# Cutting the last q loads of the first batch finer: 4, 4, 4, 2, 2 rows per partition in place of 8, 4, 2, 2

## Chip, cores and metric

The kernel runs on one core of a Trainium2 chip. The metric is the device time of one execution in microseconds (us); a median over several executions is quoted. A ratio is the mean time of one kernel's fast runs over that of the other's fast runs of the same rounds, so it is not quite the ratio of the medians beside it. "Span" is the time from the first to the last instruction in a profile; it is 1.8 us shorter than the device time.

## The reference

Two stages follow each other. Per batch (4 of them, 6144 rows, 256 columns), q and k are normed over the rows, their 256 x 256 product goes through a softmax, and v is multiplied by it. The result goes through a feed-forward stage with three input matrices and a maximum.

```python
qn = q / (norm(q, axis=1) + 1e-06);  kn = k / (norm(k, axis=1) + 1e-06)
a = softmax(kn.transpose(0, 2, 1) @ qn / tau)
x = (v @ a).reshape(B * S, D)
out = maximum(maximum(x @ w1, x @ w2), x @ w3) @ w_out
```

## The kernel before

The kernel multiplies the softmax matrix into w1, w2 and w3 first (tiles `aw`), so that v needs only one matmul per piece of the hidden layer (`h_ps`, L389) and one for the output (`o_ps`, L409). All this can start only when the first batch's softmax is known, and that needs all of its q and k. So the start of the kernel is a load stage: GpSimd issues the loads (they cast float32 to fp8 on the way), and the TensorE follows them. Sixteen DMA engines carry a load in sixteen parts, here called its shares, and a load has "landed" when its last share has. "Gram" is the product of q and k, and "backlog" is the matmuls that already have their data and still wait for their turn. Lines left out of the code are marked by dots.

```python
HEAD = 8
...
SP.dma_start(out=kf, in_=k_r[0][:, 0:HEAD, :])
for load, widths in ((load_k, [8] * 5), (load_q, [8] * 5 + [4, 2, 2])):
    g0 = HEAD if load is load_k else 0
    for w in widths:
        load(0, g0, w)          # POOL.dma_start of w rows per partition
        g0 += w
        ...
...
load_v(0)
...
for fp in range(d_ff // FT):
    load_w(fp)                  # three loads each: w1, w2, w3
```

The gram of the first batch reads q in pairs of rows; a matmul waits for the load that its rows came with. A pair of rows is two steps (j) of two matmuls:

```python
def gram(b):
    ...                                          # L165: k times k, 24 row pairs
    for tp in range(NG // 2):
        tsl = slice(2 * tp, 2 * tp + 2)
        ...
        for j in range(CC):
            ...
            PE.matmul(ps[j][:, 0:C], lhsT=qt[:, tsl, jsl], rhs=kt[:, tsl, :], ...)           # L177
            PE.matmul(ps[j][:, C:C + P], lhsT=qt[:, tsl, jsl], rhs=qt[:, tsl, jsl], ...)     # L179
```

After it come six warm-up matmuls (L469), the softmax on VectorE and ScalarE, the transposes of the first v (L372), the first products with w (L335), and then the first h matmul (L389), from where the TensorE works without a break:

```python
products(0, (0, 1))     # first half of the softmax matrix with w1, then with w2
sums(0); sums(1)
...
products(1, (0, 1))     # second half
for j in range(CC):
    products(j, (2,))   # w3
```

## Time and profile before

| | |
|---|---|
| time, median of the first three runs | 574.29 us (574.02 to 574.39) |
| the run that was profiled | 574.48 us, span 572.7 |
| TensorE busy | 97% of the span |
| idle before rows 32 to 39 of q | 2.04 us |
| gram of the first batch ends | 34.82 us |
| first h matmul (L389) starts | 38.09 us |

The prediction below shows the lines. How to read them: everything of interest happens in the first 38 us, where the TensorE follows the loads; after 38 us it waits for nothing.

### The profile page before, as it was taken

To read this page: it belongs to the slowest core of one execution; us is meant where nothing else is said; L and a number is where in the kernel's file an instruction comes from. 1 tells how busy PE (TensorE), PEld (TensorE's weight loads), DVE (VectorE), ACT (ScalarE), POOL (GpSimd) and SP (SyncE) were. 2 spreads that over 40 slices of the span, in tenths; PEclk is the share of its full clock that TensorE was granted. 3 is DMA by queue.
4 is the path that set the end of the run, shared out by engine and by line. 5 is a ranking of instruction groups with operands and counts; after the bars stand their busy time and mean duration, and the time that the engine had idled before them with its cause. 6 is when DMAs were issued, how large, how long until landed. Compare 5 with 4: busy or idle time off the path is not lost.

```text
span 572.7 us, 9441 instructions
## 1 busy us (share of the span) xinstructions
PE 553.5 (97%) x3349; PEld 330.8 (58%) x3350; DVE 411.0 (72%) x647; ACT 309.0 (54%) x539; POOL 234.5 (41%) x239
## 2 busy tenths in 40 slices
PE   3789999999999999999999999999999999999997
PEld 2665555555755555555575555555575555555566
DVE  0048777777577778777768777777868778778775
ACT  1044567767455476776545467767645444444443
POOL 2432257776740077777560048777750000000000
PEclk9999999999999999999999999999999999999999
DMA  9997998885699168885179339885537333132112
GB/s 142 106 146 124 139 236 129 152 139 108 110 107 159 57 101 160 134 145 115 58 128 149 94 82 143 155 134 93 130 79 160 75 74 111 56 101 66 56 56 76
DMA packets 76816, 65.64 MB, mean 115 GB/s; under 512 B 52448, under 2 KB 62304, under 8 KB 76640
## 3 DMA queue, kind: packets, MB, share of 16 engines
q0 software_dynamic: 18928, 26.48, 38.8%
q1 hardware_dynamic: 57696, 38.41, 23.7%
q8 instruction: 26, 0.43, 0.3%
q14 instruction: 22, 0.18, 0.1%
q10 hardware_dynamic: 144, 0.13, 0.1%
HBM read 78.64 MB, written 25.17 MB: 181 GB/s over the span
## 4 chain that ended last, share of the span: by engine, by line
PE 94%; DMA 2%; issue 2%; POOL 1%; DVE 0%; POOLq 0%
PE h_ps L389 65%; PE o_ps L409 22%; PE gram L260 3%; PE ew_ps L311 3%; DMA q_sb<-in_q_dram 2%; POOL k_sb L99 0%; PE o_ps L434 0%; POOL q_sb L102 0%; PE gram L177 0%; PE ew_ps L335 0%; PE warm_ps L469 0%; PE gram L179 0%; PE vt_ps L372 0%; PE n_ps L215 0%; DVE ht_sb L395 0%
## 5 line engine op out<-in xcount | busy, mean ns | idle before, releaser
L389 PE MATMUL h_ps<-vt_sb,aw_sb 128*128 128x512 bf16 (+1 forms) x1764 | 406.7, 375 | 0.1
L389 PEld LDWEIGHTS <-aw_sb 128*128 128x128 bf16 x1764 | 171.8, 98 | 161.3 <-DVE aw_sb L317 2.0
L394 DVE TENSOR_TENSOR s_mx<-h_ps,s_mx 128x512 bf16<-128x512 f32 (+1 forms) x294 | 198.7, 676 | 87.2 <-ACT s_mx L393 86.9
L393 ACT ACTIVATE s_mx<-h_ps 128x512 bf16<-128x512 f32 (+1 forms) x294 | 172.3, 586 | 124.9 <-PE h_ps L389 124.0
L395 DVE TENSOR_TENSOR ht_sb<-h_ps,s_mx 128x512 bf16<-128x512 f32 (+1 forms) x294 | 200.2, 681 | 31.4 <-PE o_ps L409 0.5
L203 POOL TENSOR_TENSOR acc<-acc,sq 128x768 f32<-128x768 f32 x90 | 147.6, 1650 | 70.7 <-ACT sq L197 63.1
L409 PE MATMUL o_ps<-wo_sb,ht_sb 128*128 128x256 bf16 x1128 | 153.9, 273 | 0.0
L409 PEld LDWEIGHTS <-ht_sb 128*128 128x128 bf16 x1128 | 110.4, 98 | 52.0
L412 ACT ACTIVATE o_sb<-o_ps 128x512 f32<-128x512 f32 x94 | 56.1, 597 | 85.4 <-PE o_ps L409 85.4
L110 POOL DMA_DIRECT2D v_sb<-in_v_dram x48 | 27.4, 576 | 36.5 <-DMA vt_sb<-v_sb 35.4
L197 ACT ACTIVATE sq<-q_sb 128x768 bf16<-128x768 fp8e4 x48 | 40.5, 844 | 0.0
L197 ACT ACTIVATE sq<-k_sb 128x768 bf16<-128x768 fp8e4 x48 | 40.1, 835 | 0.0
L200 POOL CAST acc<-sq 128x768 f32<-128x768 bf16 x6 | 4.9, 821 | 69.5 <-ACT sq L197 69.5
L102 POOL DMA_DIRECT2D q_sb<-in_q_dram x32 | 17.9, 567 | 4.5 <-DMA v_sb<-in_v_dram 2.5
L165 PE MATMUL kk<-k_sb 128*128 128x256 fp8e4 x48 | 7.5, 338 | 12.2 <-DVE k_sb L151 6.4
L99 POOL DMA_DIRECT2D k_sb<-in_k_dram x29 | 16.1, 556 | 2.1 <-DMA v_sb<-in_v_dram 1.3
L260 PE MATMUL gram<-k_sb,q_sb 128*128 128x512 fp8e4 x144 | 16.8, 276 | 0.0
L260 PEld LDWEIGHTS <-q_sb 128*128 128x256 fp8e4 x144 | 15.9, 136 | 0.6
L314 ACT ACTIVATE aw_sb<-ew_ps,rinv 128x384 bf16<-128x384 f32 (+1 forms) x24 | 13.1, 554 | 5.6 <-PE ew_ps L311 4.7
L311 PE MATMUL ew_ps<-w_sb,et 128*128 128x384 bf16 (+1 forms) x96 | 15.6, 313 | 0.0
L177 PE MATMUL gram<-k_sb,q_sb 128*128 128x512 fp8e4 x48 | 11.3, 334 | 3.2 <-DMA q_sb<-in_q_dram 3.2
L165 PEld LDWEIGHTS <-k_sb 128*128 128x256 fp8e4 x48 | 6.4, 182 | 13.2 <-DMA k_sb<-in_k_dram 6.7
(67 smaller groups left out, 113.1 us busy)
## 6 DMA issues: line engine op xcount, KB each, us to landing
out_dram<-o_sb SPq DMA_DIRECT2D x41, 512.0 KB, 2.9
v_sb<-in_v_dram POOLq DMA_DIRECT2D x48, 256.0 KB, 4.2
k_sb<-in_k_dram POOLq DMA_DIRECT2D x24, 192.0 KB, 5.7
q_sb<-in_q_dram POOLq DMA_DIRECT2D x24, 192.0 KB, 7.1
out_dram<-o_sb SPq DMA_DIRECT2D x13, 256.0 KB, 2.0
k_sb<-in_k_dram POOLq DMA_DIRECT2D x5, 256.0 KB, 11.1
q_sb<-in_q_dram POOLq DMA_DIRECT2D x5, 256.0 KB, 10.4
w_sb<-in_moe_w_dram POOLq DMA_DIRECT2D x9, 128.0 KB, 5.5
```

Source lines behind the costliest of these rows:

```text
L102: POOL.dma_start(out=qk[b][0][:, g0:g0 + w, :], in_=q_r[b][:, g0:g0 + w, :])
L110: POOL.dma_start(out=t, in_=v_r[gi // NCH, gi % NCH])
L197: ACT.activation(out=sq, in_=src, func=AF.Square)
L203: POOL.tensor_tensor(out=acc, in0=acc, in1=sq, op=ALU.add)
L260: PE.matmul(g[:, j * C:(j + 1) * C], lhsT=qt[:, tsl, j * P:(j + 1) * P], rhs=kt[:, tsl, :], start=(tp == 0 and j == 0), stop=(tp == NG // ...
L311: PE.matmul(ew[:, :w], lhsT=et[:, j, ic * P:(ic + 1) * P], rhs=w_sb[m][:, j, fsl], start=(j == 0), stop=(j == CC - 1))
L389: PE.matmul(t.rearrange("p (t n) -> p t n", n=P), lhsT=aw[m][:, ic, fsl], rhs=vt[:, tsl, ic, :], start=(ic == 0), stop=(ic == CC - 1))
L393: ACT.activation(out=s_mx, in_=hp[0], func=AF.Copy)
L394: DVE.tensor_tensor(out=s_mx, in0=hp[1], in1=s_mx, op=ALU.max)
L395: DVE.tensor_tensor(out=ht, in0=hp[2], in1=s_mx, op=ALU.max)
L409: PE.matmul(st["ps"][:, half], lhsT=ht[:, fc, t * P:(t + 1) * P], rhs=wo_sb[:, fc, :], start=(fc == 0), stop=(fc == FC - 1))
L412: ACT.activation(out=st["o"][:, t - 1:t + 1, :].rearrange("p t d -> p (t d)"), in_=st["ps"], func=AF.Copy)
```

## The change

The last loads make the TensorE wait for whole loads. The intent is to let it begin on rows 32 to 35 while rows 36 to 39 are still under way, so that less work is left when the last rows land.

```diff
-    for load, widths in ((load_k, [8] * 5), (load_q, [8] * 5 + [4, 2, 2])):
+    for load, widths in ((load_k, [8] * 5), (load_q, [8] * 4 + [4, 4, 4, 2, 2])):
```

## The prediction

> **What bounds the kernel now.** I read the page first, then the chain of work, then the timeline of the TensorE around the loads that the change touches, then the time from issue to landing of each single load.
>
> The page says that the TensorE is busy nearly all the time, and the chain that ended last puts 94% of the span on it and only 2% on a DMA: the wait for `q_sb`, the tensor whose loads are cut differently.
>
> ```profile
> PE 553.5 (97%) x3349; PEld 330.8 (58%) x3350; DVE 411.0 (72%) x647; ACT 309.0 (54%) x539; POOL 234.5 (41%) x239
> ...
> PE 94%; DMA 2%; issue 2%; POOL 1%; DVE 0%; POOLq 0%
> ```
>
> The same chain, in order of time, shows where those 2% lie: one piece of 13.48 us ahead of the gram matmuls of the first batch, ending at 31.88.
>
> ```profile
> 18.40 13.48 DMA q_sb<-in_q_dram
> 31.88 0.05 issue
> 31.93 0.32 PE gram L177
> ```
>
> The piece starts where the load was issued. The load itself waits in a queue behind other loads, so 13.48 us is no saving on offer. What the TensorE loses is read from its timeline, here with start, length and, in brackets, the idle time before:
>
> ```profile
> 29.67 0.22 PE L179 MATMUL gram<-q_sb 128*128 128x256 fp8e4 x1
> 31.93 0.32 PE L177 MATMUL gram<-k_sb,q_sb 128*128 128x512 fp8e4 x1 [2.04 <-DMA q_sb<-in_q_dram]
> ```
>
> It has used up rows 0 to 31 of q at 29.7 and idles 2.04 us for rows 32 to 39, the last load of 8 rows. After that it waits for nothing more: the same view shows it working from 31.93 to the end of the gram matmuls at 34.82. The waits of the TensorE after 38 us come out as an empty list, so what is won or lost before 38 us reaches the end of the kernel one to one, and nothing else is on offer.
>
> The landings, each from the view of DMA issues over a window that holds one issue only (size, then us from issue to landing): the load of rows 32 to 39, then those of 4, 2 and 2 rows, issued at 18.40, 18.92, 19.44 and 19.96.
>
> ```profile
> q_sb<-in_q_dram POOLq DMA_DIRECT2D x1, 256.0 KB, 13.5
> ...
> q_sb<-in_q_dram POOLq DMA_DIRECT2D x1, 128.0 KB, 13.5
> ...
> q_sb<-in_q_dram POOLq DMA_DIRECT2D x1, 64.0 KB, 13.6
> ...
> q_sb<-in_q_dram POOLq DMA_DIRECT2D x1, 64.0 KB, 13.7
> ```
>
> To a hundredth, from the trace's landing records: rows 24 to 31 at 28.29, 32 to 39 at 31.88, 40 to 43 at 32.42, 44 to 45 at 33.02, 46 to 47 at 33.67. Every 8-row load up to there came 2.4 to 2.5 us after the one before it; this one came 3.59 us after. The per-engine records of its landing explain that: fifteen of its sixteen shares landed between 29.82 and 30.74, and one at 31.88. At 29.88 a single packet of another queue started and took 0.97 us; the window from 29.85 to 30.9 has it:
>
> ```profile
> q8 instruction: 1, 0.02, 5.8%
> ```
>
> It is a block of instructions for the TensorE (working below), and one of the sixteen DMA engines carried it in the middle of its share of rows 32 to 39.
>
> **What the Trainium skill says.** "Runtime: NRT & Kernel Launch", section Instruction fetch mechanics: an engine's instructions come in blocks of 16 KiB, 256 instructions, over the sequencer's own DMA queue. The trace agrees: queue q8 moved 26 packets of 16,384 bytes, and 3349 + 3350 TensorE instructions over 256 make 26.2. "DMA: Bandwidth & Descriptors", section Why a DMA increments its semaphore by 16 and not by 1: a load counts as landed only when all sixteen engines have reported; the 15 + 1 shares above are just that. The same page, section Anatomy of one DMA, gives each DMA a fixed cost of about 2.0 us, mostly completion latency. This trace shows that it is not paid in series when loads queue up: the first of the sixteen shares of consecutive loads landed at 27.36, 29.82, 31.10, 31.75 and 32.39, so 8 rows took 2.46 us, 4 rows 1.28, 2 rows 0.65 and 0.64. "TensorE: Matmul & The Clock Gate", Part 1, says that the array runs at half clock until it has been busy for a few microseconds. The trace agrees: a step of two gram matmuls took 0.32 us until 26.77 and 0.167 us after, and stayed fast over the 2.04 us of idling.
>
> **The change, part by part.** One load of 8 rows becomes two of 4; the rest is as before. The order of instructions shows one more DMA issue on GpSimd (240 rows against 239), none added elsewhere, and the other engines' order unchanged apart from which of the eight DMA semaphores each wait names.
>
> *Removed.* The matmuls for rows 32 to 35 no longer wait for rows 36 to 39. Rows 32 to 35 need 1.28 us after the shares of the load before. The latest share of that one was at 28.29, so they land by about 29.57, before the instruction block at 29.88 can delay them. The TensorE runs out at 29.7, so it goes straight on. A pair of rows takes two steps of two matmuls, so rows 32 to 47 are 16 steps, 2.67 us from 31.93 to 34.60 (0.167 each), and rows 32 to 35 are 4 steps, 0.67 us. So 0.67 us of work moves from after 31.93 to before 30.4, into idle time.
>
> *Added.* One DMA. On an engine 8 rows cost 2.46 us, twice 4 rows 2.56: 0.10 us later for everything behind it in the queue, rows 36 to 39 at about 31.98, then 32.52, 33.12 and 33.77. On GpSimd one more issue, about 0.57 us; it issues that far ahead of the landings that this is hidden. With eight semaphores in turn, a load waits for the one eight before it, so the first load of v and the first three of w are issued one landing later (v at 23.4 in place of 21.2); their turn at the DMA engines comes only after 33.7, so this is hidden as well.
>
> *The gram's end.* From 31.98 + 0.05: rows 36 to 39 until 32.70, rows 40 to 43 (there at 32.52) until 33.37, rows 44 to 45 (33.12) until 33.70, rows 46 to 47 at 33.77 + 0.05, with 0.34 us of work, until 34.16, and 0.06 more of draining. Against 34.82 that is 0.6 us earlier. The end is now set by the last landing and not by the backlog.
>
> *What follows it.* Six warm-up matmuls, the transposes of v, the softmax, and the first matmuls with w. Here the timeline reads:
>
> ```profile
> 35.96 0.61 PE L372 MATMUL vt_ps<-ident,v_sb 128*128 128x128 bf16 x8
> 36.50 0.61 PE L335 MATMUL ew_ps<-w_sb,et 128*128 128x256 bf16 x4
> 36.94 0.24 PE L329 MATMUL rs_ps<-ones_c,et 128*128 128x1 bf16 x4
> 37.05 1.03 PE L335 MATMUL ew_ps<-w_sb,et 128*128 128x256 bf16 x8
> ```
>
> These come 0.6 us earlier only if their data is there. v landed at 35.00 for 35.96 (0.96 us to spare); the first w at 35.66 for 36.50 (0.84); the second at 36.31 for the third of those four matmuls, at 36.73 (0.42); the third at 36.96 for 37.48 (0.52). All of them come 0.10 later now. The tightest is the second w: 0.42 - 0.10 leaves 0.32 us. So of the 0.6 us the TensorE keeps about 0.3 and gives the rest back in a wait for w that is not there now. **Sum:** 574.29 - 0.3 = 574.0.
>
> **The rivals.** *The gain arrives whole (573.7).* It would if the second w came earlier than I reckon, for instance if splitting costs nothing on the DMA engines or the share that is late there has caught up. Against it: those loads run back to back, the DMA engines are full (the table of windows gives a DMA share of 1.05 and 1.20 for 25 to 30 and 30 to 35 us), and nothing in the change makes them faster. *A wait takes the place of the wait (574.3 or a little more).* If the split costs 0.3 us and more, or the instruction block strikes the first of the two loads or the last ones, the last rows land later and all is lost. Speaking for it: one packet moved a landing by 1.1 us here. Against it: what calls for that block is the TensorE's progress up to 29.7, which does not change. *The 2 us of the fixed cost are paid again (576).* The spacings of 0.65 us between loads of 2 rows speak against it. *The array falls back to half clock (575 to 576).* The idle stretches become shorter, not longer, so I give it little. *The wait was worth its 2.04 us (572.3).* That would need the last landing to move, which it doesn't: splitting brings nothing sooner than 33.67.
>
> **Range and chances.** The three runs of before spread 0.37 us, and my gain may be 0.0 to 0.65 with a centre at 0.3; together that makes 573.5 to 574.5 for 8 times in 10. A change by 2% would be 11.5 us, over five times the idle time at stake, so nearly all the weight is on the same: 0.99, and half a percent for either side.
>
> **What would show each step right or wrong.** In the profile after: no idle time before rows 32 to 35, or some tenths, at 29.7, and then an idle stretch of about 1.5 us before rows 36 to 39, ending near 32.0; last gram matmul over at about 34.2; a short new wait for `w_sb` of 0.2 to 0.3 us at L335; first h matmul (L389) at 37.7 to 37.9 in place of 38.09; landings of the last two rows and of w each 0.1 later. I am wrong in the removed part if the gram still ends at 34.8; wrong in the added part if the last rows land more than 0.3 later; wrong in what follows if L389 starts a full 0.6 earlier; and wrong about the bound if L389 starts earlier and the end does not.

## The result, and the profile after

| | before | changed |
|---|---|---|
| median, us | 574.15 (573.91 to 575.43, 6 runs) | 574.06 (573.90 to 575.65, 6 runs) |
| ratio | | 0.9999, 95% interval 0.9985 to 1.0013 |

The time is the same. The page's busy times and the chain, as for before:

```profile
PE 553.9 (97%) x3349; PEld 330.7 (58%) x3350; DVE 411.1 (72%) x647; ACT 309.1 (54%) x539; POOL 235.1 (41%) x240
...
PE 93%; DMA 5%; POOL 0%; issue 0%; DVE 0%; POOLq 0%
```

GpSimd has one more instruction, the extra issue. The DMA's share of the chain rose from 2% to 5% although nothing became slower. The chain in order of time tells why:

```profile
3.97 16.66 DMA q_sb<-in_q_dram
20.63 0.28 issue
20.91 12.72 DMA q_sb<-in_q_dram
33.63 0.04 issue
33.67 0.32 PE gram L177
```

It now goes through the last load of q (landed 33.63), not through the load of rows 32 to 39. That is the change at work: the gram ends on the last landing. The chain also shows something that I had not listed: the last q load is the eighth after rows 0 to 7 in the turn of eight semaphores, so it is issued only once those have landed, at 20.91. Both pieces count the whole time from issue to landing, most of which the load spends queued, so the share says nothing of what could be saved.

The timeline of the TensorE at the same place (start, length, idle time before):

```profile
30.06 0.22 PE L179 MATMUL gram<-q_sb 128*128 128x256 fp8e4 x1
31.35 0.32 PE L177 MATMUL gram<-k_sb,q_sb 128*128 128x512 fp8e4 x1 [1.07 <-DMA q_sb<-in_q_dram]
...
33.67 0.32 PE L177 MATMUL gram<-k_sb,q_sb 128*128 128x512 fp8e4 x1 [0.16 <-DMA q_sb<-in_q_dram]
```

There is no wait before rows 32 to 35 any more. The wait is now before rows 36 to 39 and half as long, and a short one stands before the last two rows. The loads of rows 32 to 35, 36 to 39, 40 to 43, 44 to 45 and 46 to 47, each from a window that holds one issue only:

```profile
q_sb<-in_q_dram POOLq DMA_DIRECT2D x1, 128.0 KB, 11.4
...
q_sb<-in_q_dram POOLq DMA_DIRECT2D x1, 128.0 KB, 13.0
...
q_sb<-in_q_dram POOLq DMA_DIRECT2D x1, 128.0 KB, 13.4
...
q_sb<-in_q_dram POOLq DMA_DIRECT2D x1, 64.0 KB, 13.5
...
q_sb<-in_q_dram POOLq DMA_DIRECT2D x1, 64.0 KB, 12.7
```

In the landing records that is 29.26, 31.30, 32.26, 32.91 and 33.63, with the instruction block starting at 29.30. The work behind the gram:

```profile
35.37 0.61 PE L372 MATMUL vt_ps<-ident,v_sb 128*128 128x128 bf16 x8
35.90 0.69 PE L335 MATMUL ew_ps<-w_sb,et 128*128 128x256 bf16 x4
36.43 0.24 PE L329 MATMUL rs_ps<-ones_c,et 128*128 128x1 bf16 x4
36.53 1.03 PE L335 MATMUL ew_ps<-w_sb,et 128*128 128x256 bf16 x8
37.52 0.38 PE L389 MATMUL h_ps<-vt_sb,aw_sb 128*128 128x512 bf16 x1
```

L389 starts at 37.52, which is 0.57 us before the 38.09 of before, and the first four products take 0.69 in place of 0.61: the wait for the second w, 0.08 us. So this pair of profiles says "0.57 us gained" while the timed runs say "nothing". That contradiction is what the experiments are for.

### The profile page after: what moved, and what is told of

The parts are those of the page before. It is cut to its first block, busy times and chain, and to the rows that moved or that the text cites. A ratio compares the mean times of both kernels' runs of the same rounds, so it can differ in the third digit from the quotient of the medians.

```text
span 572.1 us, 9442 instructions
## 1 busy us (share of the span) xinstructions
PE 553.9 (97%) x3349; PEld 330.7 (58%) x3350; DVE 411.1 (72%) x647; ACT 309.1 (54%) x539; POOL 235.1 (41%) x240
## 4 chain that ended last, share of the span: by engine, by line
PE 93%; DMA 5%; POOL 0%; issue 0%; DVE 0%; POOLq 0%
PE h_ps L389 65%; PE o_ps L409 22%; DMA q_sb<-in_q_dram 5%; PE gram L260 3%; PE ew_ps L311 3%; POOL k_sb L99 0%; PE o_ps L434 0%; PE ew_ps L335 0%; PE warm_ps L469 0%; PE vt_ps L372 0%; PE gram L177 0%; PE n_ps L215 0%; DVE ht_sb L395 0%; DVE o_sb L461 0%; PE n_ps L217 0%
## 5 line engine op out<-in xcount | busy, mean ns | idle before, releaser
L389 PE MATMUL h_ps<-vt_sb,aw_sb 128*128 128x512 bf16 (+1 forms) x1764 | 406.7, 375 | 0.1
L389 PEld LDWEIGHTS <-aw_sb 128*128 128x128 bf16 x1764 | 171.8, 98 | 161.3 <-DVE aw_sb L317 2.0
```

What stands on the lines that cost most here:

```text
L389: PE.matmul(t.rearrange("p (t n) -> p t n", n=P), lhsT=aw[m][:, ic, fsl], rhs=vt[:, tsl, ic, :], start=(ic == 0), stop=(ic == CC - 1))
```

## Experiments

All eleven runs gave correct results, and all timed executions with a recorded state are fast ones, but for the single one of base2, whose state is unknown. My theory: what counts is the start of L389; the change replaces the wait for a backlog by the wait for the last landing, and costs a little on the DMA engines. Rivals: the whole 0.57 us is the change's; nothing is; splitting a load costs much or nothing; the waits belong to the size of a load and not to the instruction block.

This is what the profiles of all runs show, in us, from the landing records and the timelines. "To the end" is from the start of L389 to the end of the span.

| kernel | block of instructions | rows 32 to 39 landed | last of q landed | gram ends | L389 | to the end |
|---|---|---|---|---|---|---|
| before, first profile | 29.88 | 31.88 | 33.67 | 34.82 | 38.09 | 534.6 |
| base1 (= before) | 29.20 | 31.21 | 33.60 | 34.20 | 37.59 | 534.6 |
| base2 (= before) | 29.39 | 31.40 | 33.49 | 34.34 | 37.61 | 534.6 |
| base3 (= before) | 29.62 | 31.62 | 33.41 | 34.55 | 37.83 | 534.6 |
| changed, first profile | 29.30 | 31.30 | 33.63 | 34.22 | 37.52 | 534.6 |
| again (= changed) | 29.41 | 31.43 | 33.89 | 34.48 | 37.78 | 534.6 |
| again2 (= changed) | 29.73 | 31.73 | 33.90 | 34.49 | 37.80 | 534.6 |
| eights | 29.77 | 31.78 | 33.52 | 35.11 | 38.38 | 534.6 |
| fours | 27.99 | 31.30 | 33.76 | 34.69 | 37.96 | 534.6 |
| tail16 | 33.73 | (16 rows) | 34.98 | 37.92 | 41.19 | 534.7 |
| pad_before | 24.08 | 31.21 | 33.72 | 34.31 | 37.70 | 534.6 |
| pad_after | 24.11 | 30.97 | 33.54 | 34.13 | 37.47 | 534.6 |
| pad_tail16 | 25.32 | (16 rows) | 33.24 | 36.17 | 39.44 | 534.7 |

The last column is the first finding: from L389 on, every one of the thirteen executions took the same time within 0.1 us (534.59 to 534.66). So the start of L389 is the time, and the rest of the document is about that column.

### The change and the kernel before, again: again, again2, base1, base2, base3

`again` and `again2` are the changed kernel without any edit; `base1`, `base2` and `base3` are the kernel before without any edit.

> The changed kernel once more, to separate its gain from the jitter of the start. My theory: counted from the landing of rows 24 to 31 (28.29 in the profile before, 28.01 in the first profile after), the first h matmul (L389) comes 0.3 us earlier than before: 9.8 us after that landing before, 9.5 after, again 9.5 here; time 0.3 us below the kernel before, ratio 0.9995. Rival one (the whole 0.57 us by which L389 moved in the first profile is the change's): 9.2 to 9.3 us and a time 0.6 below. Rival two (nothing is gained, the profile's difference is jitter of the start): 9.8 us and a ratio of 1.0000.

Measured: median 573.99 us (573.93 to 574.46), ratio 0.9993 (0.9979 to 1.0007). From the landing of rows 24 to 31 (28.14) to L389 it was 9.64 us, between my 9.5 and rival two's 9.8. The full 0.57 fell; between the other two it decided nothing.

> The kernel before, unchanged, timed against itself: the noise of a comparison, and a second profile of it. In all six profiles so far the end came 534.6 us after the first h matmul (L389), so the start of L389 is the time. The first profile of before had L389 at 38.09 and took 574.48 us, while its other runs lie around 574.1: I expect that this profile was a late one. Theory one (the place where the instruction block strikes, and the stray of the DMA engines, differ from run to run): L389 at 37.7 to 37.9 here, rows 32 to 39 landing less than 3.6 us after rows 24 to 31; ratio 1.000. Theory two (the first profile is typical): L389 at 38.0 to 38.2, rows 32 to 39 again 3.5 to 3.7 us after rows 24 to 31.

Measured: median 573.88 us, ratio to itself 0.9995 (0.9982 to 1.0007), L389 at 37.59. That is a little below the range of theory one and far from theory two's. The other sign decided nothing: rows 32 to 39 landed 3.56 us after rows 24 to 31, which fits both. The first profile of before was a late one.

> A third look at the kernel before, for the same two theories: L389 at 37.7 to 37.9 if the first profile was a late one, 38.0 to 38.2 if it is typical.

Measured: 573.98 us in one run, L389 at 37.61, again a little below the range of theory one.

> The changed kernel a third time, beside the kernel before in the same rounds, for the size of its gain. From the profiles so far, the time from the last landing of q to L389 was 3.89 and 3.89 us with the change and 4.42, 3.99 and 4.12 without: the change takes 0.1 to 0.5 there, and the extra load gives 0.05 to 0.15 back by a later last landing. So here: 3.85 to 3.95 us from the last landing to L389, idle time before rows 36 to 39 near 1.0 and a second short one before the last rows; time 0.0 to 0.2 us below before, too little for the interval. My prediction's 0.3 would be 573.75 where before has 574.05.

Measured: median 574.19 us, before 574.13 in the same rounds, ratio 0.9994 (0.9980 to 1.0008); so by the medians it is 0.06 above and not below. From the last landing to L389 3.90 us, as expected, and the idle times too, 1.2 and 0.15:

```profile
31.78 0.32 PE L177 MATMUL gram<-k_sb,q_sb 128*128 128x512 fp8e4 x1 [1.22 <-DMA q_sb<-in_q_dram]
33.95 0.32 PE L177 MATMUL gram<-k_sb,q_sb 128*128 128x512 fp8e4 x1 [0.15 <-DMA q_sb<-in_q_dram]
```

> The kernel before again, a fourth profile and a second timing against itself: 4.0 to 4.4 us from the last landing of q to L389, one idle stretch of 1.8 to 2.1 us before rows 32 to 39; L389 at 37.6 to 37.8 if the first profile was the odd one.

Measured: median 574.19 us, ratio to itself 1.0005 (0.9987 to 1.0022), L389 at 37.83 and 4.42 us from the last landing to L389, both a little above the ranges that I gave; the idle stretch of 1.73 is a little below its range. The stretch before rows 32 to 39, in base1, base2 and base3 (base2 and base3 also have one of 0.39 and 0.23 before rows 24 to 31):

```profile
31.26 0.32 PE L177 MATMUL gram<-k_sb,q_sb 128*128 128x512 fp8e4 x1 [1.97 <-DMA q_sb<-in_q_dram]
```

```profile
31.45 0.32 PE L177 MATMUL gram<-k_sb,q_sb 128*128 128x512 fp8e4 x1 [1.83 <-DMA q_sb<-in_q_dram]
```

```profile
31.66 0.32 PE L177 MATMUL gram<-k_sb,q_sb 128*128 128x512 fp8e4 x1 [1.73 <-DMA q_sb<-in_q_dram]
```

In all four profiles of before the wait is there and takes 1.7 to 2.0 us. What differs is the clock time at which it ends, 31.26 to 31.93, and with it how much backlog stands behind the last landing. Over these runs the kernel against itself moved by 0.05% up and down, and the changed kernel by 0.01% to 0.07% down; every interval takes in 1.

All executions together: of 39 of the kernel before, 33 lie under 575 us, with a mean of 574.03; of 17 of the changed one, 16, with a mean of 574.08. These means are over more than one chip, so they give no more than "equal to about 0.1 us", and that only with the executions above 575 us left out. The executions above 575 us (six and one) were 1.4 to 2.4 us longer; the padded and the 16-row kernels had such ones too. None of them of the kernel before or the changed one was profiled, so their cause stays open. Four of the seven have a granted clock of 0.997 in the records, two 1.00, and that of one (575.43 us) is not on record; the clock records of the traces know the values 1.0 and 0.5, and a mean of 0.997 over 574 us would be 3.4 us at 0.5, in which, with the 0.32 and 0.167 us per step, an estimated 1.6 us would be lost. So half clock may be behind some of them, which no run here shows. It is they that make the intervals of the ratios as wide as 0.14% and more.

### Other cuts: eights, fours, tail16

One of the three lines in each:

```diff
-    for load, widths in ((load_k, [8] * 5), (load_q, [8] * 5 + [4, 2, 2])):
+    for load, widths in ((load_k, [8] * 5), (load_q, [8] * 6)):              # eights
+    for load, widths in ((load_k, [8] * 5), (load_q, [4] * 12)):             # fours
+    for load, widths in ((load_k, [8] * 5), (load_q, [8] * 2 + [16] * 2)):   # tail16
```

> q in six loads of 8 rows: the tail uncut. My theory (the gram ends one load's work after the last landing, or one backlog after the load of rows 32 to 39): last landing at about 33.6, then 8 steps of 0.167, 1.34 us; gram end about 35.0, L389 about 38.2; time 0.2 to 0.4 us above the kernel before, as the backlog behind rows 32 to 39 hid most of what cutting the last 8 rows brings. Rival (each cut of the tail brings its rows' work): gram end at 35.8, time 1 us above.

Measured: median 574.95 us against 574.04, ratio 1.0017 (1.0003 to 1.0030). The gram's end at 35.11 and the last landing at 33.52 are as expected. The time is 0.9 us above before, more than my 0.2 to 0.4 and near the rival's 1; my figure came from the late profile of before. Against a typical L389 at 37.6 to 37.8, 38.38 is 0.6 to 0.8 later. Its waits:

```profile
31.82 0.32 PE L177 MATMUL gram<-k_sb,q_sb 128*128 128x512 fp8e4 x1 [2.06 <-DMA q_sb<-in_q_dram]
33.56 0.32 PE L177 MATMUL gram<-k_sb,q_sb 128*128 128x512 fp8e4 x1 [0.19 <-DMA q_sb<-in_q_dram]
```

So cutting the last 8 rows to 4, 2, 2, which the kernel before already does, is worth those 0.6 to 0.9 us; the cut that the change adds to it is not.

> q in twelve loads of 4 rows, to measure what a split costs on the DMA engines. My estimate of 0.10 us for a split of 8 into 4 and 4 (five of them here): last landing about 0.5 us later than before counted from the landing of rows 0 to 3 or 0 to 7, the gram then ends 0.67 us of work after it, at about 34.9, no sooner than before, and the second w lands about 0.5 later; L389 and the time 0.0 to 0.2 us above before, some 0.4 above the changed kernel. Rival (a split costs nothing, or the 0.04 us that the first shares of the changed kernel suggest): last landing within 0.2 of before, gram end at about 34.4, time 0.3 below before.

Measured: median 574.42 us against 574.15, ratio 1.0001 (0.9988 to 1.0015). Neither theory had it all. The last landing at 33.76 is 0.09 to 0.35 later than in the four profiles of before, where four loads more at my 0.10 would have made it 0.4, so a split seems to cost less than that. The first of the sixteen shares of the last q load, counted from the first share of the first k load by GpSimd, came at 24.87 us here with twelve loads and at 24.68 with the six of `eights`: 0.19 us over six splits, 0.03 each. That is one profile of each, and the same count strays by 0.23 within the kernel before (24.67 to 24.90), so by an estimate up to 0.07 each is possible. But the gram ended 0.93 us after the last landing, as its last load has 4 rows, so the time is no better:

```profile
33.80 0.32 PE L177 MATMUL gram<-k_sb,q_sb 128*128 128x512 fp8e4 x1 [0.37 <-DMA q_sb<-in_q_dram]
```

> q in loads of 8, 8, 16, 16 rows: the opposite of the change, a coarser tail. My theory (the gram ends one load's work after the last landing): the last load lands at about 33.5, its 16 rows are 16 steps of 0.167, 2.67 us, so the gram ends at about 36.2 against 34.8 before; L389 1.3 to 1.4 us later; time 1.4 us above the kernel before, ratio 1.0024. Rival one (the cut of the tail is hidden by what follows): same time. Rival two (each load costs something that is not hidden, so fewer loads are faster): time 0.2 us below.

Measured: median 576.82 us (575.80 to 577.63) against 574.15, ratio 1.0040 (1.0026 to 1.0055). The direction is my theory's; the 2.7 us are about twice the 1.4 that I gave. In the profile, which is of the longest of its runs, the last load landed at 34.98 and not at 33.5; the idle time before it:

```profile
35.03 0.32 PE L177 MATMUL gram<-k_sb,q_sb 128*128 128x512 fp8e4 x1 [1.45 <-DMA q_sb<-in_q_dram]
```

Fourteen of its shares had landed by 33.17, and two came at 34.94 and 34.98. The instruction block had started at 33.73, and I took it for the cause. The landing records say otherwise: two shares are late from rows 8 to 15 on, 8 us before the block. There they came at 25.25 and 25.31 where the other fourteen had landed by 23.01, and of rows 16 to 31 at 30.10 and 30.16 where the others had by 28.31. The TensorE waited for each of these loads:

```profile
25.35 0.48 PE L177 MATMUL gram<-k_sb,q_sb 128*128 128x512 fp8e4 x1 [1.90 <-DMA q_sb<-in_q_dram]
...
30.20 0.32 PE L177 MATMUL gram<-k_sb,q_sb 128*128 128x512 fp8e4 x1 [2.03 <-DMA q_sb<-in_q_dram]
```

The block shows up later, and on a third share: of the first load of w, thirteen shares landed by 35.12, one at 35.99 and the same late two at 36.88 and 36.91. Among the packets of the loads one of 2048 bytes, started at 21.08, took 1.75 us. What held two engines up then stays open.

These kernels give one rule, which holds in all the profiles. From the last landing of q to the end of the gram it was 0.59 to 0.60 us with 2 rows in the last load (the changed kernel, base1, both kernels padded with tails of 2), 0.93 with 4, 1.59 with 8 and 2.93 to 2.94 with 16. A row pair is two steps of 0.167, so the rows' work is 0.33, 0.67, 1.34 and 2.67, and about 0.26 is left over each time. In the kernel before a second term competes: the landing of rows 32 to 39 plus the work for 16 rows, 2.67 + 0.26 = 2.93. Its four profiles have 34.82 (31.88 + 2.94), 34.34 (31.40 + 2.94) and 34.55 (31.62 + 2.93), where that term wins, and 34.20 (33.60 + 0.60), where it doesn't.

### The block of instructions: pad_before, pad_after, pad_tail16

Each adds 32 tiny matmuls (64 TensorE instructions with their weight loads) on zeros, whose result is not read, into the idle stretches of the k phase: pad_before to the kernel before, pad_after to the changed one, pad_tail16 to the kernel of `tail16`. So the TensorE asks for its next block of instructions earlier; the loads are not touched.

```diff
+    def pad(n):
+        pad_ps = htile("pad_ps")
+        for i in range(n):
+            PE.matmul(pad_ps[:, 0:1], lhsT=warm[:, 0:P], rhs=warm[:, 0:1], start=(i == 0), stop=(i == n - 1))
...
                 PE.matmul(kk[:, jsl], ...)
+            if tp in (3, 7, 11, 15):
+                pad(8)
```

> The kernel before with 32 tiny matmuls (64 TensorE instructions, on zeros, never read) put into the idle stretches of the k phase, so that the TensorE reaches its next block of instructions 64 instructions earlier, in the rows 8 to 16 of q. The loads are those of before. My theory (the instruction block on one DMA engine made the load of rows 32 to 39 land 1.1 us late): the 16 KiB packet moves from 29.9 to 23 to 26, rows 32 to 39 land about 2.9 instead of 3.6 us after rows 24 to 31 or sooner, the wait before them falls from 2.0 to 1.0 to 1.5, the gram ends at about 34.2 in place of 34.8, L389 0.3 to 0.4 earlier: as much as the change itself. Rival (the wait is that of an 8-row load as such): wait stays at 2.0, gram end 34.8, L389 and time unchanged.

Measured: median 574.17 us against 574.15, ratio 1.0006 (0.9987 to 1.0024). The block moved to 24.08, rows 32 to 39 landed 2.52 us after rows 24 to 31 (28.69), and the wait before them fell to 0.97. The delay went with the block, to rows 16 to 23:

```profile
26.27 0.32 PE L184 MATMUL gram<-k_sb,q_sb 128*128 128x512 fp8e4 x1 [1.22 <-DMA q_sb<-in_q_dram]
...
31.26 0.32 PE L184 MATMUL gram<-k_sb,q_sb 128*128 128x512 fp8e4 x1 [0.97 <-DMA q_sb<-in_q_dram]
```

So the extra microsecond of wait is the block's and not that of an 8-row load as such. (The padding has a second effect: the steps are fast from 24.02 us on, in place of 24.90 to 26.77 in the four profiles of before. The wait before rows 32 to 39 doesn't hang on it, since in all of these the TensorE has used up rows 0 to 31 and waits for the landing. L184 is the same line of code, moved down by the edit.) It ended the gram at 34.31 as expected, but the time is not better, since the kernel before is in general near that already.

> The changed kernel with the same 64 TensorE instructions in the k phase as in the padded kernel before: the instruction block strikes at about 24 and no longer at 29.3. My theory (with the change the gram is bound by the last landing, which the block delays all the same as that DMA engine does not catch up): the wait before rows 36 to 39 falls below 0.7, gram end and L389 within 0.15 of the changed kernel's, same time: the two remedies do not add up. Rival (the block is still the bound in the changed kernel): L389 0.3 to 0.5 earlier, time 0.3 to 0.5 below the changed kernel.

Measured: median 574.14 us against 574.04, ratio 1.0000 (0.9988 to 1.0013). The wait before rows 36 to 39 fell from 1.07 to 1.22 to 0.34. The one before rows 40 to 43 grew to 0.32 from at most 0.21, and the one before the last two rows stayed at 0.15. The gram still ended 0.59 us after the last landing, as my theory has it. L389 at 37.47 is 0.05 before the first changed profile, but 0.23 before the mean of the three, near the rival's 0.3; the rival's 0.3 to 0.5 of time is not there. So the two remedies do not add up, as far as the timed runs can tell.

```profile
31.01 0.32 PE L184 MATMUL gram<-k_sb,q_sb 128*128 128x512 fp8e4 x1 [0.34 <-DMA q_sb<-in_q_dram]
...
33.59 0.32 PE L184 MATMUL gram<-k_sb,q_sb 128*128 128x512 fp8e4 x1 [0.15 <-DMA q_sb<-in_q_dram]
```

One share stays behind after the block, which I read as the DMA engine that carried it (the records don't name engines): in base1 the last share of q's last load came 0.86 us after the fifteenth (33.60 and 32.74), in pad_before, where the block had struck 5 us earlier, still 0.83 (33.72 and 32.89). It is not always so much: in the other three profiles of before it was 0.36, 0.46 and 0.06, and in the changed kernel 0.56, 0.70 and 0.54.

> The loads of 8, 8, 16, 16 rows together with the 64 TensorE instructions in the k phase. The kernel with 16-row loads alone missed what I had expected of it (L389 at 41.19 in place of 39.4): its profile shows the instruction block at 33.73, in the middle of the last load, two shares of which came 1.8 us after the others. If that is the cause, the block now strikes at 23 to 27, the last load lands at 33.4 to 33.8 in place of 34.98, the gram ends at 36.2 to 36.6, L389 comes at 39.5 to 39.9, and the time is 1.7 to 2.0 us above the kernel before (ratio 1.003), about 1 us below the unpadded one. Rival (16-row loads are late by their size): last landing again near 35, L389 at 41, ratio 1.004 to 1.005.

Measured: median 576.11 us against 574.13, ratio 1.0035 (1.0020 to 1.0050). The block moved to 25.32, and the last load landed at 33.24, 1.7 us earlier than without padding. Gram end 36.17, L389 39.44, all three just below what I gave. That refutes the rival: a load of 16 rows is not late by its size. It doesn't show that the surplus of `tail16` was the block's, though the numbers came out as I had expected of that: the two late shares of `tail16` were late 8 us before its block, and here no share of rows 8 to 15 was (the last at 23.36, the fourteenth at 23.12). So what I expected came true in its numbers, and the cause that I gave for it is refuted by the trace of `tail16`; what the true one is stays open. The median fell by only 0.7 us, and the profiled run of `tail16` was its longest.

```profile
33.28 0.32 PE L184 MATMUL gram<-k_sb,q_sb 128*128 128x512 fp8e4 x1 [1.49 <-DMA q_sb<-in_q_dram]
```

No version is faster than the kernel before: the medians of before, changed and both of them padded lie at 573.88 to 574.19 in these runs, and their last landings of q at 33.4 to 33.9.

## Why the prediction was right or wrong

The range and "the same" were right: 574.06 lies in 573.5 to 574.5. That it came so near to the 574.0 of the sum is luck: the sum started from 574.29, the median of three runs, and over all runs under 575 us the kernel before took 574.03. The gain of 0.3 us is not there: without the executions above 575 us, the timed runs allow about 0.1 either way. By its steps:

- *The bound.* Right, and shown thirteen times: 534.6 us from L389 to the end.
- *Removed: rows 32 to 35 land before the block and the TensorE goes straight on.* Right. Rows 32 to 35 landed at 29.26, 29.38 and 29.55 in the three profiles, before the block each time, and no wait precedes them. The wait before rows 36 to 39 was 1.07, 1.07 and 1.22, where I had given 1.5.
- *Added: 0.10 us later for all that follows.* Not contradicted for an undelayed DMA engine, but not shown either: the first share of the last load, counted from the first share of the first k load by GpSimd, came at 24.76 us on average without the change (24.90, 24.67, 24.71, 24.75) and at 24.85 with it (24.75, 24.90, 24.89), 0.09 more, which is less than the stray of 0.23 within the kernel before; the count over `eights` and `fours` gave 0.03 per split. For the slowest engine, which decides, the means of the last landing are 33.54 and 33.81, 0.27 more. The stray within either kernel is as large (33.41 to 33.67, 33.63 to 33.90), so I can't say how much of it is the split's. The sum also left out that the last q load itself is issued later (20.91 in place of 19.96); it queues for 12.7 us, so that needn't cost anything.
- *The gram's end: "Against 34.82 that is 0.6 us earlier."* This is the step that failed, and the main term is the 34.82. (The sum has a slip as well. It lets the gram end 0.06 us after its last steps, where the prediction's own figures for before are 34.60 for the steps and 34.82 for the end, 0.22; the changed profiles have 0.59 from the last landing to the end, and the sum 0.45. With 0.22 it gives 34.38, or 0.44 earlier in place of 0.6.) The 34.82 came from one profile, and that was of the longest of the first four runs. Over four profiles the gram of before ends at 34.82, 34.20, 34.34 and 34.55; the backlog stands 0.55, 0.00, 0.25 and 0.54 us behind what the last landing alone would give (last landing + 0.60), 0.34 on average. Take from that the 0.27 of the later last landing, and 0.07 is left; the means of the gram's end, 34.48 and 34.40, and of L389, 37.78 and 37.70, say the same. The mechanism was right; the backlog that it removes was worth about half of the 0.6 that I took, and the cost that I took at 0.10 came out at 0.27 in the means, of which an unknown part is stray.
- *What follows: a wait for the second w takes back 0.3.* It exists, at 0.08 us in all three profiles, and is smaller than predicted. It is in base1 as well, where the four products take 0.77 in place of 0.61. What decides is how long after the gram's end the second w lands: 1.95 us in the three changed profiles and 2.03 in base1, with a wait, and 1.48 to 1.77 in the other three of before, without one. So far as seen it comes with a gram that ends 0.59 to 0.60 us after the last landing (these four profiles and the two padded ones with tails of 2), with or without the change.
- *The rivals.* The gain arriving whole is what the first pair of profiles seemed to show, and it was refuted by base1 and base2. The fixed cost of 2 us per load was refuted by `fours`, with four loads more and the last landing at most 0.35 later. Half clock did not come back in the profiles: the last steps take 0.167. That splitting can't move the last landing forward was right. The rival nearest to what happened is the one in which the last rows land later and the gain is lost. One reading was too broad: "every 8-row load" came 2.4 to 2.5 us after the one before it, but one of k came 3.04 after (13.54 and 10.50).

## What to carry to other kernels

In this kernel, cutting a load finer paid only for the work that is left after the last landing; count that work for each landing and take the latest of (landing + work left), over several profiles, before giving the difference a value. When a trace seems to show a delay, look for the first load that has it: in `tail16` that cleared the suspect. One profile is one draw: compare its own time with that kernel's other runs before taking a number from it. A share of the chain that is spent in a queued load (2% here, then 5%) is not time to be saved.

## What the Trainium skill lacked or had wrong

- "Runtime: NRT & Kernel Launch", Instruction fetch mechanics, says that the cost of crossing a block boundary is "mostly hidden". Here the 16 KiB block took 0.97 us of one DMA engine that was full of the kernel's own loads, and made the load of rows 32 to 39 land 1.1 us after its other fifteen shares (31.88 and 30.74). The delay moved with the block when 64 instructions were added (24.08 in place of 29.2 to 29.9), and one share was still 0.83 us behind when q's last load landed, more than 9 us after the block (0.06 to 0.86 in the four profiles of before). The time did not change with the block's place (574.17 and 574.15), so "mostly hidden" holds for the time here; that the kernel's own loads pay for the block the page doesn't say.
- "DMA: Bandwidth & Descriptors", Anatomy of one DMA, gives each DMA about 2.0 us of fixed cost. For loads that queue up, the added time on the engines was 0.03 us per split (24.68 with six loads, 24.87 with twelve; with the stray, an estimated 0.07 at most); a sentence on queued loads would help.
- "TensorE: Matmul & The Clock Gate", Part 1, describes the half clock, and nothing here contradicts it. What can mislead is the view: the granted clock in the table of windows stood at 1.00 from 20 to 25 us, where a step took 0.32 us and not 0.167. The clock records of that trace begin only at 26.84, so for the time before, the length of the steps shows the clock and the column does not.
- No page says how far the landings, and the start of the work behind them, differ between profiles of one kernel: the same kernel had L389 at 37.59 to 38.09 and the last landing at 33.41 to 33.67.
